# A spectral mixing layer in fp32 on one core: the first batch and the first tile written in program order, two tables split on the host

## The chip, the core and the metric

The kernel runs on one core of a Trainium2 chip. Times are device microseconds (us) of one execution. The trace is of one profiled execution; its times count from the start of its span. The engines are named as in the profile: PE (TensorE, matrix products), PEld (its weight loads), DVE (VectorE), ACT (ScalarE), POOL (GpSimd), SP (SyncE, which issues most transfers).

## What is computed

Two things in a row, for 8 batches of 576 tokens and a model width of 512 (8 heads of 64):

```python
p_packed = sm_attn(p, k, v)             # 32 packing queries per head attend to 576 keys
out = sm_attn(q, p_packed, p_packed)    # 576 queries attend to the 32 packed values
X = np.fft.fft(np.fft.fft(x, axis=1), axis=2)      # x: out with its heads side by side
u = x + np.real(X)
un = (u - mean(u)) / np.sqrt(var(u) + 1e-06)
return u + np.maximum(un @ w_ch1, 0.0) @ w_ch2     # 512 -> 2048 -> 512
```

## The kernel before

**The front and the tiles.** Each batch has a front (`front(b)`): the two softmaxes for two groups of four heads (g = 0, 1), then the two Fourier transforms as products with tables of cosines and sines, up to rows of `u` in the buffer `ubuf`. A batch gives 4.5 blocks of 128 rows, so that there are nine tiles of up to four blocks. Each tile goes through the two weight products (`ffn`): 16 chunks j, each with an `up` (24 instructions at the tile's start, since its first chunk is halved; 12 otherwise, `ph`, L647), a ScalarE pass `hh` (L653) and a VectorE pass `hl` (L654), which read the one PSUM bank of `ph`, and a `down` (12 products into four banks `acc`, L664), which runs one chunk later. After each `up` and each `down` comes a `step`, into which the front of the next batch is put piece by piece.

**Numbers in two parts.** Products run in a rounded format, so each operand x is a high part (a cast on ScalarE, L99) and a low part (x less the high part, L100), and a product is three (L237 to L239). The low parts of the weights, `wr_l`, are made on GpSimd anew in each tile.

**The weights' first load.** They come as 64-bit floats. A part (half a chunk: 128x512 of `w1f` or `w2f`) is put together by one ScalarE instruction (L179) and two of VectorE (a shift L180, a shift with an or L181). Chunks 0 and 1 are made ahead of the first tile, the others in its even steps, both parts of a chunk together. The first parts land in rows of `w1f` and `w2f` that are filled later (`STG0`), the others in turn in `ubuf` and a pair of buffers `wst`.

**What sets the order.** A program that adds a scheduler places the instructions of each engine by priority and dependency, except inside `manual_schedule`, where the order on PE, DVE, ACT and POOL is that of the program. Before, everything from the second tile on (t > 0) is inside, and the first batch's front and the first tile are outside. The transfers' order on SP is the scheduler's throughout. `ORDER[b]` is the order of the front's steps: K, V, Q are loads of keys, values and queries; s (scores of one group, S of both), t or X (turned scores), p, d (packed values and their parts), q or U (query scores), e, m, a (second softmax), g (spectrum of the values), f, r, h (folded weights, their remainder, their two parts). Batch 0 has an order of its own, batch 1 another, group by group, and from batch 2 on both groups go side by side. A table per batch (`EN`, `EF`, `ES`) says which of a step's passes run on VectorE (0) and which on GpSimd (1).

**After the fold.** The folded parts `fh` (ScalarE, L479) and `fl` (VectorE, L485) and the spectrum `gh`, `gl` go into 36 products `py` and `pyr` (L237 to L239), these into `pz` and `px`, and from there VectorE makes `pe`, `qe` and the four blocks of `ubuf` (L560 to L567). `statistics` takes a block's mean (L213, VectorE), its squares (`junk`, L217, ScalarE) and the deviation (L220, VectorE; L221, GpSimd). `Turned` takes the mean off (`un`, L601), transposes on PE (`untp`, L608) and splits into `uh` and `ul`; then the tile's first `ph` can start. The remainder of a batch's tokens (`R`: one more pair `pz`, `px` and `xa`, L581 to L584) comes after that.

**Tables.** `tabC`, `tabS`, `tabR` and `tabB` come as fp32 and are split or rounded in the kernel: L128, L129 (`basis`), L99, L100 (`tbh`, `tbl`), L141, L142 (`tbr`).

Of the kernel before, what the change touches and what calls it, by code (L numbers as in the profile page):

```python
# [9 lines left out]
F32 = mybir.dt.float32  # L10
# [6 lines left out]
P = 128  # L17
S = 576
# [13 lines left out]
ES = (1, 0, 0)  # L32
# [6 lines left out]
ORDER = ("K0 I0 K1 B0 V0 V1 Q0 Q1 W0 W1 W2 W3 s0 t0 p0 d0 s1 t1 p1 q0 e0 d1 g0 q1 e1 m0 m1 a0 f0 r0 h0 a1 "  # L39
         "f1 r1 h1 g1 T0",  # L40
         "s0 s1 y y t0 y t1 y p0 y y y d0 p1 y q0 d1 y y g0 y g1 y e0 q1 e1 y m0 y m1 y a0 a1 y f0 r0 h0 y "
         "y f1 r1 h1",
# [4 lines left out]
STG0 = [-2, -2, -4, -4, -6, -6]  # L47
STG1 = [9, None, None]
LEAD = 2
# [28 lines left out]
def tile_kernel(ctx, tc, kpT, qT, v, w1, w2, tabC, tabS, tabR, tabB, tabT, sel, ident_d, out):  # L78
# [45 lines left out]
    def load_base():  # L124
        nc.sync.dma_start(sels, sel)
        st = load(tabB, [P, 2, N2], "st_base", "wst")
        h = work.tile([P, 2, N2], F32R, tag="tmp", name="base_h", bufs=3)
        nc.scalar.copy(h, st)  # L128
        nc.vector.scalar_tensor_tensor(basis, h.bitcast(F32), selC, st, ALU.mult, ALU.add)  # L129
        nc.sync.dma_start(turn, tabT)  # L130

    def load_tables():
        for t, d in enumerate((tabC, tabS)):
            st = load(d, [P, 1, KT], "st_tab", (t, 2))
            split(tbh[t], tbl[t], st[:, 0, :])
        st = work.tile([P, 2, 320], F32, tag="wst", name="st_tabr", bufs=2)
        nc.sync.dma_start(st[:101], tabR)
        for t in range(2):

            h = work.tile([P, DM], F32R, tag="tmp", name="tabr_h", bufs=3)  # L140
            nc.scalar.copy(h[:101, :320], st[:101, t, :])  # L141
            nc.vector.scalar_tensor_tensor(  # L142
                tbr[t][:101], h[:101, :320].bitcast(F32), selA[:101], st[:101, t, :], ALU.mult, ALU.add)

    sels = cpool.tile([P, 3], F32, name="sels")
    selA, selB, selC = (sels[:, i:i + 1] for i in range(3))
# [9 lines left out]
    def fetch(j, n):  # L158
        i = stages.pop(0)
        if i is None:  # L160
            st = work.tile([P, 512, 2], I32, tag="wst", name="wst", bufs=2)
        elif i < 0:
            st = spot(n, i, [P, 512, 2]).bitcast(I32)
# [3 lines left out]
        fetched[j, n] = st  # L167

    def load_weights(j):

        for n, dst in enumerate((w1f, w2f)):
            if (j, n) not in fetched:
                fetch(j, n)
            st = fetched.pop((j, n))
            low, high = st[:, :, 0], st[:, :, 1]
            c = dst[:, j, :].bitcast(I32)


            nc.scalar.activation(c.bitcast(F32), high.bitcast(F32), AF.Prelu, scale=REBIAS, alpha=-2.0 ** 32)  # L179
            nc.vector.tensor_scalar(c, c, 3, None, ALU.logical_shift_left)  # L180
            nc.vector.scalar_tensor_tensor(c, low, 29, c, ALU.logical_shift_right, ALU.bitwise_or)  # L181
# [59 lines left out]
    def front(b):  # L241
# [31 lines left out]
        def scores(*gs):  # L273
# [9 lines left out]
            tails = now["acc"][2:] if len(gs) == 2 else {gs[0]: bank("s1t")}  # L283
# [161 lines left out]
        def folded_rest(g):  # L445
# [5 lines left out]
            sm = (nc.vector, nc.gpsimd)[ES[min(b, 2)]]  # L451
# [22 lines left out]
        def folded_parts(g):  # L474
# [15 lines left out]
                 "T": lambda _: load_tables(), "B": lambda _: load_base(), "K": load_keys, "V": load_values,  # L490
                 "Q": load_queries, "I": lambda _: nc.sync.dma_start(ident, ident_d),
                 "W": lambda i: fetch(i // 2, i % 2), "D": load_weights}
        for x in ORDER[min(b, 2)].split():
# [217 lines left out]
    gen0 = front(0)  # L711
    for at in gen0:
        if at == "rest":
            break
    cur = Turned(tiles[0][1])
    for i in range(4):
        cur.less(i)
        for move in cur.moves(i):
            move()
        cur.parts(i)  # L720
    for _ in gen0:
        pass
    spare.clear()
    rest = iter(())
    for j in range(ORDER[0].count("D"), LEAD):
        load_weights(j)
    ready, splits = [], wsplits()
    next(splits)
    next(splits)
    for t, (first, tk) in enumerate(tiles):  # L730

        gen = front(t + 1) if t + 1 < B else iter(())
        ended = []

        def step(i):

            next_step()
            if t > 0 and i in (0, 2):
                next(rest, None)
            elif not ended and next(gen, None) == "rest":  # L740
                ended.append(gen)
            if t == 0 and i % 2 == 0 and i // 2 + LEAD < NJ:
                load_weights(i // 2 + LEAD)
            assert i < 2 * NJ - 1 or t + 1 >= B or ended

        nxt = Turned(tiles[t + 1][1]) if t + 1 < len(tiles) else None

        with tc.manual_schedule(engines=MANUAL) if t > 0 else nullcontext():
            ffn(first, cur, step, nxt, t + 1 >= B)
        cur, rest = nxt, gen  # L750


def _tables():
# [98 lines left out]
```

## Time and profile before

| what | us |
|---|---|
| median of 3 runs (1027.23 to 1028.67) | 1028.21 |
| the profiled execution | 1027.14 |
| its span | 1025.3 |
| span up to the first `ph` of the first tile | 62.70 |
| first tile, first `ph` to the next tile's first `ph` | 126.18 |
| second tile, the same way | 108.95 |
| rest of the span after the first tile | 836.4 |

So 1.84 us lie around the span, and the profiled execution is 1.07 us below the median. PE is busy for 978.5 us (95%) of the span, DVE for 608.8, POOL for 463.1, ACT for 425.0.

How to read it: PE is all but full from the second tile on. Its idle time lies in the first 189 us, so that stretch has to be looked at by itself: which engine works there, and what PE waits for.

### The profile page before, as it was taken

To read this page: it belongs to the slowest core of one execution; us is meant where nothing else is said; L and a number is where in the kernel's file an instruction comes from. 1 tells how busy PE (TensorE), PEld (TensorE's weight loads), DVE (VectorE), ACT (ScalarE), POOL (GpSimd) and SP (SyncE) were. 2 spreads that over 40 slices of the span, in tenths; PEclk is the share of its full clock that TensorE was granted. 3 is DMA by queue.
4 is the path that set the end of the run, shared out by engine and by line. 5 is a ranking of instruction groups with operands and counts; after the bars stand their busy time and mean duration, and the time that the engine had idled before them with its cause. 6 is when DMAs were issued, how large, how long until landed. Compare 5 with 4: busy or idle time off the path is not lost.

```text
span 1025.3 us, 14876 instructions
## 1 busy us (share of the span) xinstructions
PE 978.5 (95%) x5692; PEld 795.6 (78%) x5692; DVE 608.8 (59%) x1264; ACT 425.0 (41%) x883; POOL 463.1 (45%) x419
## 2 busy tenths in 40 slices
PE   6489889999999999999999999999999999999998
PEld 2367668878877888788887887788778888887886
DVE  3897994559465856677556846594658562114112
ACT  2556454444443434444444435444435343333322
POOL 1535635364335534454345533643355344444443
PEclk9699899999999999999999999999999999999999
DMA  8328440220023000310041002200210000001001
GB/s 329 109 64 280 157 123 1 93 96 1 1 78 111 1 1 34 108 48 1 1 140 49 1 1 93 96 0 1 82 58 0 1 26 17 0 1 43 1 1 42
DMA packets 17742, 58.64 MB, mean 57 GB/s; under 512 B 2081, under 2 KB 2465, under 8 KB 17670
## 3 DMA queue, kind: packets, MB, share of 16 engines
q1 hardware_dynamic: 17670, 57.68, 16.4%
q8 instruction: 45, 0.74, 0.3%
q14 instruction: 27, 0.22, 0.1%
HBM read 48.24 MB, written 9.44 MB: 56 GB/s over the span
## 4 chain that ended last, share of the span: by engine, by line
PE 76%; DVE 11%; ACT 5%; DMA 3%; issue 2%; POOL 2%; ACTq 0%; SPq 0%; DVEq 0%; POOLq 0%
PE ph L647 35%; PE acc L664 30%; DVE ubuf L567 2%; DMA wst<-w 2%; DVE turned L419 1%; ACT hh L653 1%; PE po L326 1%; PE s L269 1%; ACT junk L217 1%; DVE turned L415 1%; POOL wr_l L100 1%; PE e1tp L303 1%; DVE hl L654 1%; ACT wr_h L99 1%; DVE w2f L181 1%
## 5 line engine op out<-in xcount | busy, mean ns | idle before, releaser
L100 POOL TENSOR_TENSOR wr_l<-w1f,wr_h 128x512 fp32r<-128x512 f32 x144 | 190.8, 1325 | 398.9 <-ACT wr_h L99 395.1
L654 DVE SCALAR_TENSOR_TENSOR hl<-ph,hh 128x512 fp32r<-128x512 f32 x144 | 98.8, 686 | 305.3 <-ACT hh L653 305.0
L647 PE MATMUL ph<-uh,wr_h 128*128 128x512 f32 (+1 forms) x580 | 231.5, 399 | 11.8 <-DVE hl L654 9.6
L100 POOL TENSOR_TENSOR wr_l<-w2f,wr_h 128x512 fp32r<-128x512 f32 x144 | 192.4, 1336 | 91.9 <-ACT wr_h L99 91.9
L664 PE MATMUL acc<-wr_l,hh 128*128 128x512 f32 x576 | 227.0, 394 | 3.0 <-POOL wr_l L100 3.0
L647 PE MATMUL ph<-uh,wr_l 128*128 128x512 f32 (+1 forms) x580 | 229.3, 395 | 0.4 <-POOL wr_l L100 0.4
L647 PE MATMUL ph<-ul,wr_h 128*128 128x512 f32 (+1 forms) x580 | 229.3, 395 | 0.2 <-DVE ul L100 0.2
L664 PE MATMUL acc<-wr_h,hh 128*128 128x512 f32 x576 | 227.8, 396 | 0.0
L664 PE MATMUL acc<-wr_h,hl 128*128 128x512 f32 x576 | 226.2, 393 | 0.0
L653 ACT ACTIVATE hh<-ph 128x512 fp32r<-128x512 f32 x144 | 85.8, 596 | 285.6 <-PE ph L647 285.4
L647 PEld LDWEIGHTS ph<-uh,wr_h 128*128 128x128 f32 x580 | 109.9, 190 | 44.9 <-DVE hl L654 9.8
L647 PEld LDWEIGHTS ph<-uh,wr_l 128*128 128x128 f32 x580 | 110.0, 190 | 24.7 <-POOL wr_l L100 0.8
L664 PEld LDWEIGHTS acc<-wr_l,hh 128*128 128x128 f32 x576 | 108.2, 188 | 26.8 <-POOL wr_l L100 5.4
L647 PEld LDWEIGHTS ph<-ul,wr_h 128*128 128x128 f32 x580 | 110.0, 190 | 23.9 <-issue 1.7
L664 PEld LDWEIGHTS acc<-wr_h,hh 128*128 128x128 f32 x576 | 108.2, 188 | 23.5 <-ACT w2f L179 0.8
L664 PEld LDWEIGHTS acc<-wr_h,hl 128*128 128x128 f32 x576 | 108.2, 188 | 23.1
L99 ACT CAST wr_h<-w2f 128x512 fp32r<-128x512 f32 x144 | 89.4, 621 | 9.4 <-PE ph L647 7.8
L99 ACT CAST wr_h<-w1f 128x512 fp32r<-128x512 f32 x144 | 88.4, 614 | 8.0 <-PE ph L647 3.1
L217 ACT ACTIVATE junk<-ubuf,stat 128x512 f32<-128x512 f32 x36 | 25.8, 718 | 77.3 <-DVE stat L213 77.3
L608 PE MATMUL untp<-ident,un 128*128 128x128 f32 x144 | 37.2, 273 | 1.9 <-DVE stat L220 1.7
L100 POOL TENSOR_TENSOR gl<-turned,gh 128x516 fp32r<-128x516 f32 x16 | 25.2, 1573 | 22.1 <-ACT gh L99 22.1
L567 DVE SCALAR_TENSOR_TENSOR ubuf<-qe,pe 128x512 f32<-128x512 f32 x32 | 34.6, 1115 | 0.5
(199 smaller groups left out, 1292.8 us busy)
## 6 DMA issues: line engine op xcount, KB each, us to landing
kp<-kpT SPq DMA_DIRECT2D x16, 608.0 KB, 4.9
out<-ubuf SPq DMA_DIRECT2D x36, 256.0 KB, 2.1
vt<-v SPq DMA_DIRECT2D x14, 640.0 KB, 4.7
wst<-w SPq DMA_DIRECT2D x17, 512.0 KB, 4.0
qt<-qT SPq DMA_DIRECT2D x14, 576.0 KB, 4.8
ubuf<-w SPq DMA_DIRECT2D x9, 512.0 KB, 4.6
w1f<-w SPq DMA_DIRECT2D x3, 512.0 KB, 11.1
w2f<-w SPq DMA_DIRECT2D x3, 512.0 KB, 11.2
```

Of the source, the lines that this page charges most:

```text
L99: nc.scalar.copy(hi, src)
L100: (lo_eng or nc.vector).tensor_tensor(lo, src, hi.bitcast(F32), ALU.subtract)
L181: nc.vector.scalar_tensor_tensor(c, low, 29, c, ALU.logical_shift_right, ALU.bitwise_or)
L217: nc.scalar.activation(junk, u, AF.Square, bias=st[:, 1:2], scale=-1.0, accum_out=st[:, 2:3])
L269: nc.tensor.matmul(res[g][c][at, :w.stop - w.start], lhs(g, h), rhs(g, h, w), start=True, stop=True, tile_position=(r, h * NPK))
L303: nc.tensor.transpose(tp[g][:, c * P:(c + 1) * P], e1s[g][:, c * P:(c + 1) * P], ident)
L567: nc.vector.scalar_tensor_tensor(u_of[key], qe, sign, pe, ALU.mult, ALU.add, accum_out=stat_of[key][:, 0:1])
L608: nc.tensor.transpose(tp[:, c * P:(c + 1) * P], un[:, c * P:(c + 1) * P], ident)
L647: nc.tensor.matmul(ph[:, t], l[:, c * P:(c + 1) * P], r[:, c, t], start=(k == 0), stop=(k == 11))
L653: nc.scalar.activation(hh[:, :T], ph[:, :T], AF.Relu)
L654: nc.vector.scalar_tensor_tensor(hl[:, :T], ph[:, :T], 0.0, hh[:, :T].bitcast(F32), ALU.max, ALU.subtract)
L664: nc.tensor.matmul(acc[i], l[:, w], r, start=(j == 0 and k == 0), stop=(j == NJ - 1 and k == 2))
```

## The change

Four things change together.

1. **The scheduler's part ends.** `manual_schedule` now spans everything, so that PE, DVE, ACT and POOL run the program's order from the first instruction on. Batch 0 gets an order of its own with both groups side by side, and batch 1 the one that all later batches have. `ES` is now per group: of batch 0, group 0's remainder is folded on POOL, group 1's on DVE.
2. **Tables.** High and low parts of the tables are made on the host. `basis`, `tbh`, `tbl` and `tbr` are loaded as they are, by seven transfers that POOL issues (an fp32 source into a rounded tile); six instructions of ACT and DVE for each kind go.
3. **Weights.** Parts are counted by one index m in the order of their use. Three are made ahead of the first tile, one in each of its steps: part i + 3 in step i, its transfer issued in step i - 2 (or, for nine, ahead of the tile). The high half (ACT) comes at the start of a step, the low half (DVE) at its end.
4. **The remainder of batch 0** moves into the first tile's steps 0 and 2, where later batches have it.

```diff
-ES = (1, 0, 0)
+ES = ((1, 0), (0, 0), (0, 0))
-ORDER = ("K0 I0 K1 B0 V0 V1 Q0 Q1 W0 W1 W2 W3 s0 t0 p0 d0 s1 t1 p1 q0 e0 d1 g0 q1 e1 m0 m1 a0 f0 r0 h0 a1 "
-         "f1 r1 h1 g1 T0",
+ORDER = ("K0 K1 I0 V0 V1 Q0 Q1 B0 L0 W0 W1 W2 W3 W4 W5 W6 W7 W8 S X p0 p1 d0 d1 U e0 e1 g0 g1 A0 m0 m1 a0 "
+         "a1 A1 f0 r0 h0 f1 r1 h1 D0",
-LEAD = 2
+LEAD = 3
     def load_base():
+        nc.gpsimd.dma_start(basis, tabB)
+        nc.sync.dma_start(turn, tabT)
+
+    def load_tables():
         nc.sync.dma_start(sels, sel)
         for t in range(2):
+            nc.gpsimd.dma_start(tbh[t], tabs[:, t, 0, :])
+            nc.gpsimd.dma_start(tbl[t], tabs[:, t, 1, :])
+            nc.gpsimd.dma_start(tbr[t][:101], tabR[:, t, :])
...
+    wparts = [(0, 0), (0, 1), (1, 0)] + [x for j in range(2, NJ) for x in ((j, 0), (j - 1, 1))] + [(NJ - 1, 1)]
...
+    def load_high(m):
+        if m < len(wparts):
+            j, n = wparts[m]
+            nc.scalar.activation((w1f, w2f)[n][:, j, :], fetched[m][:, :, 1].bitcast(F32), AF.Prelu,
+                                 scale=REBIAS, alpha=-2.0 ** 32)
+
+    def load_low(m):
+        if m < len(wparts):
+            j, n = wparts[m]
+            c = (w1f, w2f)[n][:, j, :].bitcast(I32)
             nc.vector.tensor_scalar(c, c, 3, None, ALU.logical_shift_left)
-            nc.vector.scalar_tensor_tensor(c, low, 29, c, ALU.logical_shift_right, ALU.bitwise_or)
+            nc.vector.scalar_tensor_tensor(c, fetched[m][:, :, 0], 29, c, ALU.logical_shift_right, ALU.bitwise_or)
...
-        for x in ORDER[min(b, 2)].split():
+        for x in ORDER[min(b, 1)].split():
...
+    def begin():
+        rest = front(0)
+        for at in rest:
+            if at == "rest":
+                break
+        next(splits)
+        cur = Turned(tiles[0][1])
+        for i in (0, 2):
+            for k in (i, i + 1):
+                cur.less(k)
+            for k in (i, i + 1):
+                for move in cur.moves(k):
+                    move()
+            for k in (i, i + 1):
+                cur.parts(k)
+        load_high(2)
+        load_low(1)
+        load_low(2)
+        next(splits)
+        spare.clear()
+        return cur, rest
...
+                if t == 0:
+                    if i + LEAD + 2 not in fetched:
+                        fetch(i + LEAD + 2)
+                    load_high(i + LEAD)
+                if i in (0, 2):
                     next(rest, None)
                 elif not ended and next(gen, None) == "rest":
                     ended.append(gen)
-            if t == 0 and i % 2 == 0 and i // 2 + LEAD < NJ:
-                load_weights(i // 2 + LEAD)
+                if t == 0:
+                    load_low(i + LEAD)
```

Three places show how rows move. The first is DVE at the end of batch 0's front, from the last pair of passes on the first two blocks (`ubuf`, with the numbers of the blocks' statistics) to the next blocks'. Before:

```order
L567 SCALAR_TENSOR_TENSOR ubuf_86,stat_515<-qe_512,pe_503 128x512
L567 SCALAR_TENSOR_TENSOR ubuf_86,stat_517<-qe_512,pe_503 128x512
L213 TENSOR_SCALAR stat_515<-stat_515 128x1
L181 SCALAR_TENSOR_TENSOR w2f_83<-w2f_83 128x512
L213 TENSOR_SCALAR stat_517<-stat_517 128x1
L601 TENSOR_SCALAR un_576<-ubuf_86,stat_515 128x512
L220 TENSOR_SCALAR stat_515<-stat_515 128x1
L560 TENSOR_TENSOR pe_550<-px_543,spec0_534 128x512
L220 TENSOR_SCALAR stat_517<-stat_517 128x1
L563 TENSOR_TENSOR qe_559<-px_552,spec1_541 128x256
```

And now (L208 and L215 are L213 and L220 of before):

```order
L562 SCALAR_TENSOR_TENSOR ubuf_86,stat_515<-qe_512,pe_503 128x512
L562 SCALAR_TENSOR_TENSOR ubuf_86,stat_517<-qe_512,pe_503 128x512
L208 TENSOR_SCALAR stat_515<-stat_515 128x1
L215 TENSOR_SCALAR stat_515<-stat_515 128x1
L208 TENSOR_SCALAR stat_517<-stat_517 128x1
L215 TENSOR_SCALAR stat_517<-stat_517 128x1
L555 TENSOR_TENSOR pe_550<-px_543,spec0_534 128x512
L558 TENSOR_TENSOR qe_559<-px_552,spec1_541 128x256
```

The mean of the second block and everything of the next two blocks now stand behind the first block's deviation; the passes `un` stand behind all four.

The second place is PE at the very start: scores (`s1t`, `s`), turned scores (`e1tq`, `e1tp`) and packed values (`po`) of batch 0. Before:

```order
L269 MATMUL s1t<-kp 32x64 x4
L269 MATMUL s_117<-kp 32x512 x4
L269 MATMUL s1t<-kp 32x64 x4
L306 MATMUL e1tq<-ident,e_131 64x128
L269 MATMUL s_186<-kp 32x512
L303 MATMUL e1tp<-ident,e_131 128x128 x4
L269 MATMUL s_186<-kp 32x512 x3
```

And now:

```order
L264 MATMUL s1t<-kp 32x64 x8
L264 MATMUL s_129<-kp 32x512
L264 MATMUL s_130<-kp 32x512
L264 MATMUL s_129<-kp 32x512
L264 MATMUL s_130<-kp 32x512
```

The two groups' products alternate, so that the first of them needs the keys of both groups.

The third place is DVE in the first tile, about its eighth to tenth chunk, around the passes `hl`. Before:

```order
L481 SCALAR_TENSOR_TENSOR xl<-eo,xh 128x256
L483 TENSOR_TENSOR ol<-eo,oh 128x256
L181 SCALAR_TENSOR_TENSOR w1f<-ubuf,w1f 128x512
L654 SCALAR_TENSOR_TENSOR hl<-ph,hh 128x512
L485 TENSOR_TENSOR fl<-f,fh 128x776
L180 TENSOR_SCALAR w2f<-w2f 128x512
L180 TENSOR_SCALAR w1f<-w1f 128x512
L181 SCALAR_TENSOR_TENSOR w2f<-wst,w2f 128x512
L100 TENSOR_TENSOR yl<-py,yh 128x258 x2
```

And now:

```order
L392 TENSOR_TENSOR s_1019<-s_1019,d_1226 128x576
L175 TENSOR_SCALAR w1f<-w1f 128x512
L176 SCALAR_TENSOR_TENSOR w1f<-wst,w1f 128x512
L420 TENSOR_TENSOR s_1019<-s_1019,z_1225 128x576
L422 STREAM_TRANSPOSE a<-s_1019 128x576
L175 TENSOR_SCALAR w2f<-w2f 128x512
L176 SCALAR_TENSOR_TENSOR w2f<-ubuf,w2f 128x512
L649 SCALAR_TENSOR_TENSOR hl<-ph,hh 128x512
```

Now two parts (L175 with L176, once each per step) stand between every two passes `hl`, up to step 28.

## Rows read from the trace of the kernel before

**Rows 1.** Busy time by stretch: length, busy us (instructions) per engine, granted clock, DMA.

```profile
0.00:62.70 62.70, 36.37 (x301) 24.59 (x301) 43.43 (x107) 28.61 (x66) 20.66 (x49) 0.84 0.52 183
62.70:188.88 126.18, 114.69 (x632) 89.87 (x630) 97.81 (x199) 61.27 (x122) 62.95 (x53) 0.95 0.38 125
188.88:297.83 108.95, 108.12 (x661) 88.95 (x660) 71.15 (x152) 47.12 (x100) 49.26 (x43) 1.00 0.13 45
```

**Rows 2.** Timeline, scores: start, duration, engine, line, operation, count [idle before <-releaser].

```profile
4.95 1.93 PE L269 MATMUL s<-kp 64*32 64x512 f32 x8
6.71 0.44 PE L269 MATMUL s1t<-kp 64*32 64x64 f32 x8
...
193.51 1.06 PE L269 MATMUL s<-kp 64*32 64x512 f32 x16
```

**Rows 3.** Timeline, TensorE, the last query scores of batch 0.

```profile
22.50 1.04 PE L269 MATMUL s2T<-w2f,ppT 64*32 64x512 f32 x8
```

**Rows 4.** Timeline, VectorE, batch 0: one of four spectrum products, the last fold.

```profile
20.84 0.70 DVE L415 TENSOR_TENSOR turned<-pg,turn 128x516 f32<-128x516 f32 x1 [0.35 <-PE pg L411]
...
44.49 0.97 DVE L485 TENSOR_TENSOR fl<-f,fh 128x776 fp32r<-128x776 f32 x1 [1.48 <-ACT fh L479]
```

**Rows 5.** Timeline, TensorE, the products after the fold: the first, the last, the next.

```profile
39.60 0.58 PE L237 MATMUL py<-gh,fh 128*128 128x258 f32 x1 [15.12 <-ACT fh L479]
...
48.76 0.42 PE L239 MATMUL py<-gh,fl 128*128 128x258 f32 x1
48.97 0.42 PE L237 MATMUL pyr<-gh,fh 128*99 128x258 f32 x1
...
49.37 0.28 PE L239 MATMUL pyr<-gh,fl 128*99 128x258 f32 x1
49.49 0.28 PE L237 MATMUL pz<-yh,tbh 128*128 128x258 f32 x1
```

**Rows 6.** Timeline, end of batch 0's front: statistics of a block, the first tile's start.

```profile
60.19 0.15 DVE L213 TENSOR_SCALAR stat<-stat 128x1 f32<-128x1 f32 x1
...
61.06 0.19 ACT L217 ACTIVATION_READ_ACCUMULATOR junk<-ubuf,stat 128x1 f32 x1
...
62.70 0.36 PE L647 MATMUL ph<-uh,wr_h 128*128 128x256 f32 x1
```

**Rows 7.** Waits of TensorE in the first tile: us in total, times, longest.

```profile
PE ph L647 <- DVE hl L654: 9.6, 3, 4.4
```

**Rows 8.** Groups by line, VectorE, 70 to 188 us: busy, mean ns, idle before.

```profile
L180 DVE TENSOR_SCALAR w2f<-w2f 128x512 int32<-128x512 int32 x14 | 9.0, 641 | 4.3 <-ACT w2f L179 4.3
...
L180 DVE TENSOR_SCALAR w1f<-w1f 128x512 int32<-128x512 int32 x13 | 7.2, 551 | 2.7 <-ACT w1f L179 2.7
L181 DVE SCALAR_TENSOR_TENSOR w2f<-wst,w2f 128x512 int32<-128x512 int32 x9 | 8.6, 955 | 0.2
...
L181 DVE SCALAR_TENSOR_TENSOR w1f<-ubuf,w1f 128x512 int32<-128x512 int32 x5 | 3.4, 688 | 0.1
```

**Rows 9.** Timeline of a later tile, VectorE and one TensorE row, chunks without a wait.

```profile
453.40 0.69 DVE L397 TENSOR_TENSOR s<-s,d 128x576 f32<-128x576 f32 x1
454.13 0.76 DVE L425 TENSOR_TENSOR s<-s,z 128x576 f32<-128x576 f32 x1
...
455.63 0.65 DVE L654 SCALAR_TENSOR_TENSOR hl<-ph,hh 128x512 fp32r<-128x512 f32 x1
...
457.37 0.39 PE L647 MATMUL ph<-uh,wr_h 128*128 128x512 f32 x1
...
461.64 1.45 DVE L437 TENSOR_TENSOR eo<-a 128x287 f32<-128x287 f32 x1
...
465.30 0.54 DVE L455 TENSOR_TENSOR f<-eo 128x45 f32<-128x45 f32 x4
...
477.49 0.68 DVE L654 SCALAR_TENSOR_TENSOR hl<-ph,hh 128x512 fp32r<-128x512 f32 x1
```

**Rows 10.** The table `turn`, its one transfer from SP: us from issue to landing.

```profile
DMA to landing us min/median/max: 5.9/5.9/5.9
```

More of the change, by code (lines that the diff above doesn't have):

```diff
@@ L124, in load_base @@
     def load_base():
[L125 to L129, printed above, removed]
+        nc.gpsimd.dma_start(basis, tabB)
         nc.sync.dma_start(turn, tabT)
     def load_tables():
[L133 to L137, printed above, removed]
-        for t in range(2):
[L140 to L148, printed above, removed]
+        nc.sync.dma_start(sels, sel)
+        for t in range(2):
+            nc.gpsimd.dma_start(tbh[t], tabs[:, t, 0, :])
+            nc.gpsimd.dma_start(tbl[t], tabs[:, t, 1, :])
+            nc.gpsimd.dma_start(tbr[t][:101], tabR[:, t, :])
+    sels = cpool.tile([P, 1], F32, name="sels")
+    selB = sels[:, 0:1]
     fetched = {}
@@ L280, in keys_of @@
                 return kps[g][side(g, h):side(g, h) + D, h // 2, w]
-            tails = now["acc"][2:] if len(gs) == 2 else {gs[0]: bank("s1t")}
+            tails = now["acc"][2:] if b > 0 else {g: bank("s1t") for g in gs}
             sc = narrow(gs, lambda g, h: keys_of(g, h, slice(S, S + NPK)), keys_of, "s1", tails)
@@ L709, in tile_kernel @@
     tiles = [(i, keys[i:i + 4]) for i in range(0, len(keys), 4)]
[L711 to L726, printed above, removed]
-    ready, splits = [], wsplits()
-    next(splits)
@@ L729, in tile_kernel @@
[L729 to L741, printed above, removed]
-            if t == 0 and i % 2 == 0 and i // 2 + LEAD < NJ:
-                load_weights(i // 2 + LEAD)
-            assert i < 2 * NJ - 1 or t + 1 >= B or ended
-        nxt = Turned(tiles[t + 1][1]) if t + 1 < len(tiles) else None
-        with tc.manual_schedule(engines=MANUAL) if t > 0 else nullcontext():
+    ready, splits = [], wsplits()
@@ new lines, in tile_kernel, with step @@
+    with tc.manual_schedule(engines=MANUAL):
+        cur, rest = begin()
+        for t, (first, tk) in enumerate(tiles):
+            gen = front(t + 1) if t + 1 < B else iter(())
+            ended = []
+            def step(i):
+                next_step()
+                if t == 0:
[3 more added lines that the diff above has]
+                if i in (0, 2):
+                    next(rest, None)
+                elif not ended and next(gen, None) == "rest":
+                    ended.append(gen)
+                if t == 0:
+                    load_low(i + LEAD)
+                assert i < 2 * NJ - 1 or t + 1 >= B or ended
+            nxt = Turned(tiles[t + 1][1]) if t + 1 < len(tiles) else None
@@ L749, in tile_kernel @@
             ffn(first, cur, step, nxt, t + 1 >= B)
-        cur, rest = nxt, gen
+            cur, rest = nxt, gen
 def _tables():
@@ L812, in _prepare @@
     }
[L813 removed]
+    for n, t in zip(("tabs", "tabR", "tabB", "tabT", "sel", "ident_d"), _tables()):
         arrays[n] = t
```

50 lines of the change are left out of this document (24 added, 26 removed).

## The prediction

> **What bounds the kernel now.** I read the stretches first [rows 1]. From the first tile's end on nothing is to be had: the second tile takes 108.95 us with TensorE busy for 108.12, and the change leaves every row there as it is. The 836.4 us behind the first tile are taken as they are. The first two stretches hold the loss: 62.70 us up to the first `ph`, in which VectorE works for 43.43 and TensorE for 36.37, and a first tile of 126.18, 17.2 longer than the second. The timeline then says who holds TensorE. In the front it is the chain through VectorE: TensorE idles 15.12 us until the first folded part is there [rows 5], and it then runs at the lower of its two levels (1.2 GHz): one product starts 0.21 us after the other at 48.76, and 0.12 after it at 49.37 [rows 5]. In the first tile it is `hl`, 9.6 us in three waits [rows 7]: `ph` has one bank, and the next `up` waits until VectorE has read it. The rest of the 17.2 is slow clock around these waits (granted share 0.95, [rows 1]).
>
> So there are two terms: the first `ph` moves, and the first tile becomes a tile like the others with weight parts in it.
>
> **The change part by part.**
>
> *First `ph`, step 1: to the query scores.* Before, they end at 23.54 [rows 3]. Now the first product waits for both groups' keys, 6.71 instead of 4.7; in return 16 products of both groups take as long as 8 (1.06 us for 16 at the fast level, 1.93 for 8 at the slow one [rows 2]). At best the whole 1.93 is won, at worst nothing, because group 0 no longer runs ahead. I take the middle: 22.6.
>
> *Step 2: to the last `fl`.* Before it ends at 45.46 [rows 4], 21.9 after the query scores, with VectorE all but full. Now all four spectrum products stand behind the query scores, where two stood ahead of them: 2 x 0.70 [rows 4] = 1.4. Smaller rows change sides, each under 1 us by its duration: group 0's query transposes and group 1's remainder come in, a weight shift and the wait for GpSimd's second remainder go out. I take +1.1 for these, between -1.5 and +2. The last `fl` ends at 22.6 + 21.9 + 1.4 + 1.1 = 47.0. The rows on the tables cost nothing here: they ran after this point, under TensorE's products.
>
> *Step 3: `py`.* In program order the sixth product already needs group 1's `fl`, so 31 of 36 are left at 47.0. At 0.21 each that is 6.5, at 0.12 it is 3.7. Before, TensorE had idled, took up work at 39.60 and came to the fast level near 49.4. It will have idled longer here; I let it turn fast at 51.5: 21 products in 4.5 and 10 in 1.2, end at 52.7 (50.7 to 53.5). Before: 49.65.
>
> *Step 4: from there to `ph`.* Before 13.05 us. Now, with `after` at work only inside tiles, each block's statistics stand in line: mean, squares on ScalarE, deviation, then the next block. One block takes 60.19 to 61.25 [rows 6] and some 0.15 to hand over, 1.2. The chain, counted from the last `pyr`: last split and both `pz` 2.0, `pe`, `qe` and the first two blocks 2.75, so 4.75; two statistics 2.4, 7.15; the next `pz` copies stand behind ScalarE's squares, then the same passes again, 2.95, 10.1; two statistics, 12.5; `un` of blocks 0 and 1 and their transposes, split on ScalarE and VectorE, then `un` of 2 and 3, which stand behind the second `ul`: 4.5, 17.0; their transposes, with TensorE having idled for 8 us and so slow, 1.9, 18.9. (All products of that step stand ahead of the first `ph`.) The scheduler had laid the weight shifts, `xa` and `un` between these. `xa` and its two followers leave this stretch and come back inside the tile, where every later tile has them in its 108.95; nothing is booked twice.
>
> First `ph`: 52.7 + 18.9 = 71.6, **8.9 later**. Bounds: 50.7 + 17 = 67.7 to 53.5 + 20.5 = 74. The first `up` then starts slow: 24 half products at 0.21 instead of 0.12 would be 2.2; I take 1.0.
>
> *First tile.* Without parts it would take 108.95. In it 29 parts are put together. VectorE's two rows have means of 0.55 to 0.64 and 0.69 to 0.96 in the first tile before [rows 8], together 1.24 to 1.60; since rows start about 0.15 before their forerunner's end, 1.1 to 1.45 in a row, and I take 1.30. The whole is 38 us, and a later tile leaves VectorE 108.95 - 71.15 = 37.8 [rows 1]. But the room isn't where the parts are. Between 450.0 and 477.5 of a later tile, five chunks, VectorE never waits: `hl` follows on the row before it [rows 9], and TensorE runs at its 5.44 per chunk. Its only slack is that `hl` at 455.63 ends 1.1 before the next `ph` at 457.37 [rows 9]. Ten parts fall there, 13.0 us. Batch 1 has some of that work on GpSimd, as before: two scalings of group 0 (0.69 and 0.76) and its fold, 461.64 to 465.30 = 3.7 [rows 9], together 5.2. Left: 13.0 - 5.2 - 1.1 - 0.2 of idle = **6.5 us of waits**. At 1.1 a part it is 4.5, and below that if the collisions with GpSimd fall on other rows. If GpSimd comes late with its steps so that VectorE waits for them, the 5.2 don't count: 11.7. The waits are of 1 to 2.5 us, and after waits of 4 us TensorE's clock fell before; I take 1.2 for slow stretches. The tile: 108.95 + 6.5 + 1.2 = 116.65, **9.5 less** than 126.18.
>
> ScalarE's part of this (one row per part, under 0.7) is hidden: it is busy for 47.12 of 108.95 [rows 1]. It now stands ahead of `hh` in ScalarE's order, so a late transfer would hold `hh` and TensorE behind it; a part's transfer has two steps, some 6.8 us.
>
> *Tables.* Seven transfers are issued by GpSimd ahead of its first work in the front, which comes near 16.5 us. The trace has no transfer from GpSimd. The nearest row is SyncE's `turn`, 5.9 from issue to landing [rows 10]: if GpSimd only issues, the price is nothing, if it were held for each landing, 41 us, with its first work 25 late. I take nothing, since SyncE's own issues follow each other without waiting for landings.
> The Trainium skill (SBUF — State Buffer, SBUF: two separate sides) has a rule against such a move: a transfer issued by GpSimd needs descriptors written through a port that VectorE's two-port passes lock, and it gives 3.1 us for one that alone takes 0.62. No run here shows a transfer under such a lock; by that figure seven would end near 22 and the sum would be some 6 us longer.
>
> **The sum.** Span: 71.6 + 1.0 + 116.65 + 836.4 = 1025.65, 0.35 more than 1025.3. With the 1.84 around the span the profiled execution would take 1027.5; the median of runs lies 1.07 above the profiled one, so **1028.6**. About 0.2% (2.1 us) is what a measurement of this kernel can tell from no change, so this is no change: two terms of nine us against each other.
>
> **The rivals.**
>
> *Fewer collisions, faster.* If VectorE and GpSimd meet less than taken, both terms shrink: a pass like the one at 461.64 takes 1.45 where its twins without GpSimd take a third. For: group 1's remainder leaves GpSimd in the front. Against: in the first tile GpSimd has more to do than in later ones. Step 2 at 45.4, `py` to 51.0, `ph` at 69.9 (+7.2), first `up` +0.5; the tile with 3 of waits and 0.4 of slow clock 112.35 (-13.8): 6.1 less, **1022.1**.
>
> *VectorE's line holds the first tile, slower.* One mechanism, in the eighth to twelfth chunk: in program order VectorE waits at its transpose `a` for GpSimd's scaling of group 0, which stands behind two `wr_l`, and ten parts queue behind that. For: no slack there in a later tile [rows 9]. Against: before, batch 1 had the same division. Waits 11.7, slow clock 2.5, tile 123.15 (-3.0); with +8.9 and +1.0 it is 6.9 more, **1035.1**. It decides from waits of about 8 us on.
>
> *GpSimd's transfers hold its first work.* Priced above: 25 us, some 1054. For: nothing in the trace; that SyncE issues freely speaks against.
>
> **How the numbers follow.** Forecast 0.38, collisions 0.33, line 0.26, transfers 0.03. Of the forecast's 0.38, some 0.08 lie outside the 0.2%, half on each side. So faster 0.37, within 0.2% 0.30, slower 0.33. The range reaches down past the second case by 2 (step 1 and step 3 at their low ends) and up past the third by 2: 1020 to 1037. The likeliest case's own range is 1025 to 1032.
>
> **What would show it.** The first `ph` near 71.6 us, four statistics in a row with VectorE idle on ScalarE's squares ahead of it, and `py` still slow at 50. In the tile: waits for `hl` in the eighth to twelfth chunk, of 6 us in sum and 1 to 2.5 each, none of over 4. The prediction is wrong if the first `ph` comes before 67 (steps 2 to 4) or after 75, if the first tile is under 112 or over 122, or if a later tile leaves 108.95.

## The result, and the profile after

The changed kernel takes 1031.63 us in the median of six runs (1031.27 to 1033.40), the kernel before 1028.55 on the same chip (1027.23 to 1029.06, six runs). The ratio is 1.0036 with a 95% interval of 1.0023 to 1.0049: slower by more than the 0.2% that can be told from no change. The forecast of 1028.6 was no change, with a range of 1020 to 1037.

Two terms of several us stand against each other, as forecast, though both came out smaller (8.9 later and, with the slow first `up`, 8.5 shorter were forecast). The busy times by stretch (length, busy us and instructions of PE, PEld, DVE, ACT, POOL, granted clock, DMA share, GB/s) answer to [rows 1]:

```profile
69.98:192.03 122.05, 113.26 (x674) 91.97 (x673) 105.57 (x201) 64.83 (x131) 59.80 (x52) 0.97 0.41 130
192.03:301.00 108.97, 108.16 (x662) 88.95 (x661) 71.90 (x153) 47.14 (x100) 50.34 (x44) 1.00 0.13 45
0.00:69.98 69.98, 28.59 (x257) 21.36 (x257) 40.93 (x110) 23.07 (x52) 21.71 (x44) 0.73 0.46 168
```

The first `ph` comes 7.28 us later (69.98 after 62.70), the first tile is 4.13 shorter (122.05 after 126.18), so that the second tile starts 3.15 later, which is the whole difference of the medians. The profiled execution took 1031.47 and is 4.33 above that of before; the other 1.2 us lie behind the first tile (837.67 after 836.42), where no chunk is more than 0.06 us longer and half of it comes behind the last `up`. In the traces of the experiments below this stretch takes 836.8 to 837.7, so that the profiled run of before was at its low end, and nothing points to the change there.

The front, in the timeline of after (start, duration, engine, line; L208 and L215 are L213 and L220 of before, L596 is L601, L642 is L647), to be read beside [rows 3 to 6]:

```profile
19.83 1.05 PE L264 MATMUL s2T<-w2f,ppT 64*32 64x512 f32 x1
...
45.40 0.97 DVE L480 TENSOR_TENSOR fl<-f,fh 128x776 fp32r<-128x776 f32 x1 [0.24 <-ACT fh L474]
...
49.16 0.42 PE L234 MATMUL pyr<-gh,fl 128*101 128x258 f32 x1
...
49.69 0.28 PE L234 MATMUL py<-gh,fl 128*128 128x258 f32 x1
...
51.48 0.28 PE L234 MATMUL pyr<-gh,fl 128*99 128x258 f32 x1
...
56.68 0.15 DVE L208 TENSOR_SCALAR stat<-stat 128x1 f32<-128x1 f32 x1
57.77 0.15 DVE L215 TENSOR_SCALAR stat<-stat 128x1 f32<-128x1 f32 x1 [0.94 <-ACT junk L212]
58.87 0.15 DVE L215 TENSOR_SCALAR stat<-stat 128x1 f32<-128x1 f32 x1 [0.88 <-ACT junk L212]
59.13 0.69 DVE L555 TENSOR_TENSOR pe<-px,spec 128x512 f32<-128x512 f32 x1
...
64.00 0.87 DVE L596 TENSOR_SCALAR un<-ubuf,stat 128x512 f32<-128x512 f32 x2
64.62 1.94 PE L603 MATMUL untp<-ident,un 128*128 128x128 f32 x8 [7.65 <-DVE un L596]
...
69.98 0.56 PE L642 MATMUL ph<-uh,wr_h 128*128 128x256 f32 x1
```

VectorE waits for ScalarE's squares ahead of each deviation (0.94 and 0.88 in the first pair, the same in the second), and TensorE has been idle for 7.65 us when the transposes start.

The waits of TensorE in the first tile of after (us in total, times, longest) answer to [rows 7]:

```profile
PE ph L642 <- ACT wr_h L97: 6.3, 3, 2.5
PE ph L642 <- DVE s L369: 1.4, 1, 1.4
PE ph L642 <- DVE hl L649: 0.6, 1, 0.6
PE acc L659 <- POOL wr_l L98: 0.5, 1, 0.5
```

The first row has to be read with care. It names ScalarE's `wr_h`; the timeline around the first of the three waits, with the first rows of the other two, shows who really came last for `ph`:

```profile
125.48 0.69 DVE L176 SCALAR_TENSOR_TENSOR w2f<-wst,w2f 128x512 int32<-128x512 int32 x1
126.09 0.68 DVE L649 SCALAR_TENSOR_TENSOR hl<-ph,hh 128x512 fp32r<-128x512 f32 x1
126.26 0.62 ACT L97 CAST wr_h<-w2f 128x512 fp32r<-128x512 f32 x1 [2.11 <-DVE w2f L176]
126.92 0.47 PE L642 MATMUL ph<-uh,wr_h 128*128 128x512 f32 x1 [1.76 <-ACT wr_h L97]
...
134.69 0.63 PE L642 MATMUL ph<-uh,wr_h 128*128 128x512 f32 x1 [2.05 <-ACT wr_h L97]
...
149.96 0.47 PE L642 MATMUL ph<-uh,wr_h 128*128 128x512 f32 x1 [2.50 <-ACT wr_h L97]
```

This `wr_h` is made from `w2f`, which `ph` doesn't read. `hl` ends at 126.77, and `ph` starts 0.15 later; at the wait that the profile does give to `hl` (113.66) the distance is 0.14, and at the other two of these waits it is 0.14 and 0.15 as well. Both `hl` and `wr_h` had waited for the same weight part. So the waits are for `hl`, in all four cases.

### The profile page after: what moved, and what is told of

Same layout as the page of the kernel before. It is cut to its first block, busy times and chain, and to the rows that moved or that the text cites. A ratio compares the mean times of both kernels' runs of the same rounds, so it can differ in the third digit from the quotient of the medians.

```text
span 1029.7 us, 14881 instructions
## 1 busy us (share of the span) xinstructions
PE 970.0 (94%) x5692; PEld 794.6 (77%) x5692; DVE 615.2 (60%) x1271; ACT 423.2 (41%) x878; POOL 463.5 (45%) x414
## 4 chain that ended last, share of the span: by engine, by line
PE 79%; DVE 11%; ACT 4%; issue 3%; POOL 2%; DMA 0%; SPq 0%; ACTq 0%; POOLq 0%; DVEq 0%
PE ph L642 36%; PE acc L659 31%; DVE ubuf L562 2%; DVE turned L414 1%; ACT hh L648 1%; ACT junk L212 1%; PE po L321 1%; DVE turned L410 1%; POOL wr_l L98 1%; PE py L234 1%; PE e1tp L298 1%; PE untp L603 1%; PE s L264 1%; PE py L232 1%; PE py L233 1%
## 5 line engine op out<-in xcount | busy, mean ns | idle before, releaser
L642 PE MATMUL ph<-uh,wr_h 128*128 128x512 f32 (+1 forms) x580 | 231.4, 399 | 10.2 <-ACT wr_h L97 6.3
L642 PE MATMUL ph<-uh,wr_l 128*128 128x512 f32 (+1 forms) x580 | 229.0, 395 | 0.0
L642 PE MATMUL ph<-ul,wr_h 128*128 128x512 f32 (+1 forms) x580 | 228.8, 394 | 0.0
L642 PEld LDWEIGHTS ph<-uh,wr_h 128*128 128x128 f32 x580 | 110.2, 190 | 44.8 <-ACT wr_h L97 7.5
L642 PEld LDWEIGHTS ph<-uh,wr_l 128*128 128x128 f32 x580 | 110.1, 190 | 24.2 <-POOL wr_l L98 0.2
L642 PEld LDWEIGHTS ph<-ul,wr_h 128*128 128x128 f32 x580 | 110.2, 190 | 21.7
L232 PE MATMUL py<-gh,fh 128*128 128x258 f32 x64 | 19.0, 298 | 20.8 <-ACT fh L474 20.8
L98 DVE TENSOR_TENSOR ul<-untp,uh 128x512 fp32r<-128x512 f32 x36 | 24.1, 687 | 20.4 <-ACT uh L97 20.4
```

The lines of the kernel that those rows point to most:

```text
L98: (lo_eng or nc.vector).tensor_tensor(lo, src, hi.bitcast(F32), ALU.subtract)
L232: nc.tensor.matmul(o, lh, rh, start=first, stop=False)
L642: nc.tensor.matmul(ph[:, t], l[:, c * P:(c + 1) * P], r[:, c, t], start=(k == 0), stop=(k == 11))
```

## The experiments

In what follows, a wait is sized by the distance from one `up` or `down` to the next, beside the same distance in the second tile, and j counts the chunks from 0. In after the first tile is 13.1 us longer than the second:

| where | us more |
|---|---|
| first `up` and the steps up to the second | 2.0 |
| ahead of j = 4, query transposes | 1.1 |
| `hl`, ahead of j = 6, 8, 9, 11, with the products right after | 0.9, 2.3, 2.2, 2.8 |
| the slow `up` of j = 9 | 1.7 |

In the first row, the first `up` takes 4.45 us up to the next step's first product, 1.7 more than in the second tile, at a granted clock of 0.62. But the clock isn't what sets this row: in e2_stats_un (below) the first `up` takes 3.6, and the second still comes 7.38 after the first instead of 7.67. The score products between them wait in both: seven of the sixteen start together 0.05 to 0.06 us behind the end of ScalarE's first copy `spec` (76.63 after 76.58 in after, 70.29 after 70.23 in e2_stats_un), which speaks for ScalarE's line; no run takes that line away.

The theory: the front is late because statistics stand in line, and the tile is longer by weight parts that stand in front of `hl` where VectorE is full. The rivals: the front hangs on TensorE's clock and on the line of splits; the tile hangs on VectorE's waits for GpSimd.

**Statistics put off (e1_stats).** Of the kernel after, with

```diff
+        if steps[0] is None:
+            due.append((2 + key[2], squares))
+            due.append((4 + key[2], deviation))
+            return
         after(1, squares)
```

> The changed kernel, with squares and deviations of batch 0's first four blocks put off into steps 1 to 4 of the first tile (the means stay). Theory (statistics in line): the second pair's pe, now at 59.13 us, starts at 56.9, and un, now at 64.0, another 2.1 earlier: the first ph comes at 65.7 us (65 to 66.5) instead of 69.98, the first tile stays at 122 (up to 123 if the squares hold hh on ScalarE), the span falls by 4.3 (3.3 to 4.7). Rival (the slow TensorE and the line of splits on ScalarE and VectorE set that stretch, the statistics only fill its gaps): first ph not before 68.5, span less by under 1.5.

Measured: first `ph` at 65.97, first tile 121.8, 1027.20 us (ratio to before 0.9989, 0.9976 to 1.0002), 4.4 less than after. The theory holds, to 0.3 us.

**`un` moved up (e2_stats_un).**

```diff
             for k in (i, i + 1):
                 for move in cur.moves(k):
                     move()
-            for k in (i, i + 1):
+            if i == 0:
+                continue
+            for k in range(4):
                 cur.parts(k)
```

> As e1_stats, and un of blocks 2 and 3 with their transposes stands ahead of the splits uh, ul of blocks 0 and 1. Theory: the second eight transposes now start 3.7 us after the first eight (68.36 and 64.62), because un 2 stands behind the second ul; they will start some 1.8 after. First ph 1.9 earlier than in e1_stats, at 63.8 (63.2 to 64.6), span 1.9 less than e1_stats. Rival (ScalarE's four uh in a row hold the first ph): gain under 0.7.

Measured: all 16 transposes now run as one group, and the first `ph` is at 63.92:

```profile
61.09 3.18 PE L607 MATMUL untp<-ident,un 128*128 128x128 f32 x16 [3.34 <-DVE un L600]
...
63.92 0.56 PE L646 MATMUL ph<-uh,wr_h 128*128 128x256 f32 x1
```

1025.46 us (0.9975, 0.9963 to 0.9987). These two edits give back 6.1 of the 7.3 us.

**Twelve parts left out (e4_leave).** VectorE's two instructions are not issued for the parts of steps 12 to 23, so that those weights lack their low bits.

```diff
-                if t == 0:
+                if t == 0 and not 12 <= i <= 23:
                     load_low(i + LEAD)
```

> The changed kernel, with VectorE's two instructions left out for the parts of steps 12 to 23 (their low bits are missing from the weights; transfers and ScalarE's half stay). Theory: no wait for hl from chunk 7 on, no slow clock there: tile 112.5 us (111.5 to 113.5). Rival (GpSimd's steps or the transfers hold the line): tile 117 or more.

Measured, in one execution: first tile 114.77, 7.3 less, no wait for `hl` behind j = 6 and no slow `up`.

```profile
PE acc L659 <- POOL wr_l L98: 1.6, 2, 1.1
PE ph L642 <- DVE hl L649: 0.6, 1, 0.6
```

It stayed above the expected 113.5 since a wait came forth that had been hidden: 1.1 us for GpSimd's `wr_l`, in the `down` ahead of j = 10. So twelve parts cost 7.3 us there, not 12 x 1.3, and what is left to GpSimd's lateness alone (the rival) is this 1.1.

**Parts made earlier in the tile (e3_early).** The place of each part comes from a list: one more in steps 1, 3, 5, 7, 9, none in 12 to 16.

```diff
-                    load_low(i + LEAD)
+                    for m in PLAN[i]:
+                        load_low(m)
```

> The changed kernel, with the same parts made earlier: one more part in each of steps 1, 3, 5, 7 and 9, none in steps 12 to 16, so that seven instead of twelve parts fall into steps 12 to 23 (transfers land in four more places). Theory (VectorE is full there, each part costs its 1.3 us): in chunks 6 to 11 TensorE's waits for hl, 8.2 us more than in the second tile plus 1.7 of slow clock, fall to 2 and 0; the tile takes 114.5 us (113 to 117) instead of 122.05. Rival (VectorE's line held by GpSimd's late steps in the eighth to tenth chunk, whatever parts stand there): tile 119 or more. Rival (extra parts in the early chunks cost what they save later): 120 to 123.

Measured: 1031.44 us (1.0031, 1.0017 to 1.0045), the time of after; the profiled run was the longest of its ten (1035.37), and in its trace the tile takes 125.5. The theory's number fell. By the median the tile is as long as in after, which is the last rival's number (120 to 123); the trace's own 125.5 lies above it, and the first rival's 119 or more is not set apart by either (e4_leave does that). The waits of the tile in that trace show why:

```profile
PE ph L652 <- ACT wr_h L107: 2.8, 2, 2.4
PE ph L652 <- DVE hl L659: 2.7, 1, 2.7
PE acc L669 <- POOL wr_l L108: 1.6, 2, 1.1
PE s2Tt L274 <- DMA qt<-qT: 1.3, 1, 1.3
PE ph L652 <- DVE s L379: 1.0, 1, 1.0
```

The 2.7 us wait is now ahead of j = 6, behind the added parts: chunks 3 to 5 had no room either. And pulling the weights' transfers forward made the queries of batch 1 land late.

**Parts made in the front's gaps (e5_plan).** On e2_stats_un, six parts ahead of the tile, one more in steps 0 to 3, none in 9 and 12 to 18.

```diff
+            if n < 2:
+                load_low(n + 1)
...
-        load_high(2)
-        load_low(1)
-        load_low(2)
+        for m in (3, 4, 5):
+            load_low(m)
```

> As e2_stats_un (first ph 63.92, first tile 122.92), with the weight parts moved to where VectorE waits: parts 1 and 2 behind the two yr of batch 0's front, 3 to 5 behind the last ul, so that the tile starts with six parts made; then one per step, one more in steps 0 to 3, none in steps 9 and 12 to 18 (transfers land in four more places). Theory (waits come from parts in full stretches, chunks 6 to 11; the early room is in the front and in chunks 0 and 1, not in chunks 3 to 5 where e3_early put them): first ph 63.9 (63.5 to 64.5), first tile 115 (113.5 to 117), time 1017.5. Rival (VectorE is as full in the early chunks, what is saved late is paid early): tile 119 or more, a wait of over 2 us in chunks 2 to 5.

Measured: 1027.02 us (0.9988, 0.9978 to 0.9999), first `ph` 65.32, first tile 122.5, as long as without the plan. The rival's number (119 or more) came, but not its mechanism: not one wait for `hl` is left, and others have taken their place.

```profile
PE acc L673 <- POOL wr_l L108: 3.1, 4, 1.1
PE po L335 <- DMA vt<-v: 2.2, 1, 2.2
PE ph L656 <- DVE s L383: 1.4, 1, 1.4
```

The values of batch 1 landed late, behind weight parts: SyncE issues five between 69.26 and 78.69 and the second half of the values at 79.11, where in after none is issued from 50 us until both halves of the values are (77.78). And TensorE's granted clock was 0.63 in the 4.6 us after that wait (4.0 us in all). The parts of the last chunks, now two steps ahead of their use instead of three, came just late (3.9 us, around j = 11 and in the last two chunks).

**The clock in the front (e6_warm, e11_warm_py).** Products that nobody reads fill TensorE's idle time.

```diff
+        for _ in range(n):
+            nc.tensor.matmul(o[:, :256], lhs, rhs, start=True, stop=True)
```

> As e2_stats_un, with 157 more products on TensorE whose results nobody reads, in its idle stretches of batch 0's front: 110 behind the spectrum products, 22 behind xh of group 0, 25 behind the last px. Theory (the low clock level after idling costs py, the transposes and the first up): py at 0.12 us instead of 0.21 a product, its end at 50.3 instead of 52.53, transposes and first up at the fast level, first ph at 61.3 (60.5 to 62), first up 4.6 instead of 5.35, span 3.4 less (2.5 to 4.5). Rival (these stretches hang on VectorE and ScalarE, TensorE's level is covered): first ph 63.3 or later, span less by under 1. Rival (the added products run at the low level and hold py): first ph later than 64.5.

Measured: first `ph` at 63.08, 0.8 earlier, and 1025.79 us (0.9976, 0.9966 to 0.9986), the time of e2_stats_un. That is far from the theory's 61.3 and close to the first rival's 63.3: `py` was still slow for the most part, because TensorE idled again between the two groups' folded parts:

```profile
45.69 0.58 PE L236 MATMUL py<-gh,fh 128*128 128x258 f32 x1 [2.23 <-ACT fh L483]
...
47.07 0.42 PE L236 MATMUL py<-gh,fh 128*128 128x258 f32 x1
47.28 0.42 PE L237 MATMUL py<-gl,fh 128*128 128x258 f32 x1
```

So the next kernel fills this wait too, with 17 more.

> As e6_warm, with 17 more unread products in the 2 us in which TensorE waits between group 0's and group 1's folded parts, where its clock fell again in e6_warm. Theory (with the level up, the 18 products from 46.7 on that still took 0.21 us take 0.12): py's last product ends at 50.6 instead of 52.42, first ph at 61.4 instead of 63.08, time 1.7 less. Rival (behind py the line of VectorE and ScalarE sets the time anyway): first ph 62.5 or later.

```profile
43.16 2.18 PE L243 MATMUL fill<-xh,pph 128*128 128x256 f32 x17
45.57 0.39 PE L236 MATMUL py<-gh,fh 128*128 128x258 f32 x1 [0.23 <-ACT fh L483]
...
46.92 0.28 PE L237 MATMUL py<-gl,fh 128*128 128x258 f32 x1
47.03 0.28 PE L238 MATMUL py<-gh,fl 128*128 128x258 f32 x1
...
50.26 0.28 PE L238 MATMUL pyr<-gh,fl 128*99 128x258 f32 x1
```

Measured: one product starts 0.12 us after the other, the last ends at 50.54, the first `ph` is at 61.21; 1023.45 us (0.9955, 0.9941 to 0.9968). The theory holds: the low level in `py` cost 1.9 us of the front.

**The front left to the scheduler (e7_schedfront).**

```diff
-    with tc.manual_schedule(engines=MANUAL):
-        cur, rest = begin()
+    cur, rest = begin()
+    with tc.manual_schedule(engines=MANUAL):
```

> The changed kernel, with batch 0's front left to the scheduler (same order of emission), and only the first tile and what follows in program order. Theory (the front loses 7.3 us to program order, above all to the statistics in line; the tile's gain is independent of it): first ph 63 us (62 to 64.5), first tile 122 (121 to 123.5), time 1024 (1022.5 to 1026). Rival (the two groups side by side make the front late, however it is ordered): first ph 67 or later, time 1028 or more.

```profile
57.62:184.00 126.38, 115.69 (x681) 94.15 (x682) 106.86 (x209) 65.58 (x133) 60.00 (x54) 0.96 0.38 126
```

Measured: 1021.75 us (0.9937, 0.9922 to 0.9953), faster than before and after. The first `ph` came at 57.62, earlier than expected, because the scheduler put the first five of the 24 products of the first `up` ahead of the transposes of blocks 2 and 3; the tile's length isn't comparable for that. The second tile's start is: 184.00, against 192.03 for after and 188.88 for before. So the program order of the front costs 8.0 us (9.9 by the medians; the profiled run was the longest of its four), and the rest of the change gains 4.9 (6.2 by the medians, 1027.99 of before and 1021.75).

**Tables alone (e8_tables).** The kernel before, with the tables of after.

> The kernel before with only the tables changed: parts made on the host, seven transfers issued by GpSimd, the rows of basis, tbh, tbl and tbr gone from ScalarE and VectorE. Theory (they ran beside TensorE's products): first ph 62.7 within 0.7, time within 2 us of before. Rival (VectorE's 3.3 us of tbl and tbr, 45.4 to 48.5, hold the first yl and all behind it): first ph 60 to 61.5, time 1.5 to 3 less. Rival (transfers from GpSimd hold its first work): first ph 64 or later.

Measured: 1027.19 us over ten runs (0.9991, 0.9976 to 1.0006): no change that can be told. The profiled run is the fastest of the ten (1024.11), so its first `ph` at 61.76 decides nothing within 1 us. That leaves the rival on VectorE's 3.3 us (1.5 to 3 less) open: the interval reaches down to 2.5 less. In after's trace the rival on GpSimd's transfers is out: issuing one takes 0.5 to 0.8 us, and GpSimd's first work on the front starts when VectorE's `pp` releases it.

```profile
1.26 0.79 POOL L123 DMA_DIRECT2D basis<-tabB  x1 [0.43 <-issue]
...
5.25 0.55 POOL L131 DMA_DIRECT2D tbr<-tabR  x1
...
15.13 0.61 POOL L329 TENSOR_TENSOR bd<-pp,bmask 128x256 f32<-128x256 f32 x1 [9.33 <-DVE pp L326]
```

**A better plan for the parts (e9_sched_plan, e10_sched_plan_b).** Both on e7_schedfront, with six parts in the front, transfers of parts 9 to 12 issued there, and a lead that never falls under 4. They differ in which steps get a second part and which none: (0, 1, 2) and (12, 13, 14, 15, 18) in e9, (0, 1) and (13, 15, 17, 19) in e10.

> As e7_schedfront (batch 0's front left to the scheduler, first tile in program order; first ph 57.62, first down 68.15, second tile's first ph 184.0), with six parts made in the front, one more part in each of steps 0, 1 and 2, and none in steps 12 to 15 and 18, so that the lead never falls under 4; the transfers of parts 9 to 12 are issued in the front, where the queues are idle. Theory (a wait for hl shrinks by 1.3 us for each part taken out of the two steps ahead of it, and without waits of 2 us the clock stays up): the waits ahead of chunks 8 and 9 go (4.5), the one ahead of chunk 11 halves (1.3), 1.7 of slow clock goes: second tile at 176.5 (175.5 to 179), time 1014.5 (1013 to 1017). Rival (as in e5_plan, VectorE running ahead makes others late: batch 1's values land late, GpSimd's low parts, the last weights): 181 or later, time 1018.5 or more.

> As e9_sched_plan, but one more part in steps 0 and 1 only, and none in steps 13, 15, 17 and 19: every chunk from the seventh to the tenth is relieved of one of its two parts instead of some of both. Theory (each part is worth its 1.3 us where the wait is longer than that): the waits ahead of chunks 8, 9 and 11 shrink by 1.3 each (3.9), slow clock 1.7 goes: second tile at 178.4 (177.5 to 180), time 1016. Rival (others become late): 181 or later.

Measured: e9 1019.73 us (0.9921, 0.9908 to 0.9933), second tile at 180.91; e10 1019.19 us (0.9913, 0.9900 to 0.9927), second tile at 179.94. e10's second tile came into its range at the edge (177.5 to 180), but its time is 3.2 above the expected 1016; e9 fell short by 4.4, near its rival's 181. The waits of e9 ahead of j = 8 and 9 are gone, but there the values land 1.2 us late again, and TensorE waits 1.8 us for a `wr_l` that GpSimd reaches later; e10 has that wait too (1.7).

```profile
82.27 0.90 PE L331 MATMUL po<-vt,e1T 128*32 128x64 f32 x40 [1.23 <-DMA vt<-v]
...
128.68 0.50 PE L669 MATMUL acc<-wr_l,hh 128*128 128x512 f32 x1 [1.76 <-POOL wr_l L108]
```

e10 beats the kernel before by 0.87%.

**Parts in pairs (e12_pairs).** Undoes the spreading over half chunks: both parts of a chunk in the even step, four ahead of the tile. (In this kernel one of the last parts is overwritten in its landing place before it is read, so that half a chunk of weights is wrong; this lies behind the waits spoken of.)

```diff
-                if t == 0:
-                    load_low(i + LEAD)
+                if t == 0 and i % 2 == 0:
+                    load_low(i + 4)
+                    load_low(i + 5)
```

> The changed kernel, with both parts of a chunk made in the even steps, as the kernel before had it, in place of one part in each step (four instead of three ahead of the tile; more places for the transfers, issued two steps ahead as in the changed kernel, so that none lands late). Theory (what counts is VectorE's work between two hl, and two steps, so two parts, stand between them either way): first ph 70 (69.5 to 70.7), first tile 122 (120.5 to 123.5), time 1031.4 within 1.5. Rival (two parts in a row hold hl as they did before, in waits of about 4 us): tile 125 or more, time 1034 or more.

Measured: 1037.91 us (1.0100, 1.0077 to 1.0123), first `ph` 70.20, first tile 128.1. The theory fell, the rival's number held, though not by waits of 4 us for `hl`. The largest wait is for the query transposes, ahead of j = 4, in front of which now two parts stand:

```profile
100.94 0.41 DVE L176 TENSOR_SCALAR w1f<-w1f 128x512 int32<-128x512 int32 x1
101.39 0.69 DVE L177 SCALAR_TENSOR_TENSOR w1f<-w2f,w1f 128x512 int32<-128x512 int32 x1
101.99 1.50 DVE L176 TENSOR_SCALAR w2f<-w2f 128x512 int32<-128x512 int32 x1
103.53 0.69 DVE L177 SCALAR_TENSOR_TENSOR w2f<-w1f,w2f 128x512 int32<-128x512 int32 x1
104.13 0.37 DVE L370 STREAM_TRANSPOSE s<-s2Tt 128x64 f32<-128x64 f32 x2
...
104.52 0.61 PE L643 MATMUL ph<-uh,wr_h 128*128 128x512 f32 x1 [3.59 <-DVE s L370]
```

`hl` isn't the only pass that TensorE waits for: the tail of the query scores lies in `ph`'s bank too. Behind it the clock fell (1.6 us in that `up`, 1.5 in that of j = 6). So, in program order, one part per half chunk is worth some 6 us of the first tile.

## Why the prediction was right, and where not

| step | predicted | measured |
|---|---|---|
| 1, query scores end | 22.6 | 20.88 |
| 2, last `fl` ends | 47.0 | 46.37 |
| 3, last `py`, `pyr` ends | 52.7 | 51.76 |
| 4, from there to the first `ph` | 18.9 | 18.2 |
| first `ph` | 71.6 | 69.98 |
| first tile, with the slow first `up` | 117.65 | 122.05 |
| rest of the span | 836.4 | 837.67 |

*Step 1* was out of its bounds: it is 2.7 us earlier than before, where 1.93 was the most thought possible. The bound took only the products; with both groups side by side their passes on VectorE and ScalarE come closer together as well: ScalarE's first pass `e` of group 1 starts 1.0 us after that of group 0 (10.51 after 9.54), before 6.7 (14.64 after 7.99).

*Step 2* lost what step 1 had won: 25.5 us after the query scores, where 24.4 was predicted, just over the upper bound of 25.3. That the two came out only 0.6 early together is luck: the errors, -1.7 and +1.1, stand against each other.

*Step 3* was right in that `py` starts at the low level, which e11_warm_py prices at 1.9 us. But the clock rose at 49.4, as in before, though TensorE had idled longer (18.78 us instead of 15.12); the 51.5 that was put in for this, and the sign that `py` is still slow at 50, did not come.

*Step 4* was right, in size and cause: 18.2 for 18.9, and its inner marks (the first two blocks, each pair of statistics, the second `un`) lie within 0.3 us of the sum's. e1_stats takes 4.0 us off with the statistics alone, e2_stats_un another 2.1 with `un` that stood behind `ul`.

*First tile.* It took 122.05, just over the 122 that the prediction had named as the sign of being wrong. The kind of the waits was right: four waits for `hl`, idle for 0.6 to 2.5 us each, none over 4, the last three ahead of j = 8, 9 and 11. The tile is 4.4 longer than forecast; sized as above, these rows hold it but for 0.1:

| term | predicted | measured |
|---|---|---|
| waits for `hl` in the eighth to twelfth chunk | 6.5 | 7.3 |
| wait for `hl` ahead of j = 6 | 0 | 0.9 |
| wait for the query transposes ahead of j = 4 | 0 | 1.1 |
| slow clock behind the waits | 1.2 | 1.7 |
| first `up` and the steps behind it | 1.0 | 2.0 |

So the balance over the five full chunks was 0.8 off. The step that failed is that the waits were looked for in these five alone, as if the other chunks, which have room in sum, could have none: 2.0 us came there. A wait comes from the work ahead of one particular pass. Inside the five chunks too, nothing was waited for ahead of j = 7 and 10, and over 2 us each ahead of j = 8, 9 and 11; e3_early and e12_pairs made waits of 2.7 and 3.6 us ahead of j = 6 and 4 by parts put there. The term for the first `up` was half the measured size, and its cause, the slow clock, accounts for 0.3 of the 2.0 by e2_stats_un.

How the parts come to cost what they do can be seen in VectorE's and GpSimd's rows of after:

```profile
115.01 1.46 POOL L98 TENSOR_TENSOR wr_l<-w2f,wr_h 128x512 fp32r<-128x512 f32 x1 [0.95 <-POOL wr_l L98]
115.34 1.68 DVE L176 SCALAR_TENSOR_TENSOR w1f<-wst,w1f 128x512 int32<-128x512 int32 x1
117.46 0.69 DVE L176 SCALAR_TENSOR_TENSOR w2f<-wst,w2f 128x512 int32<-128x512 int32 x1
```

The same pass takes 0.69 alone and 1.68 when GpSimd has begun a pass of its own; it then ends 0.55 us after GpSimd's (117.02 after 116.47, and likewise 0.55 at 112.92 and 122.87). The Trainium skill (SBUF — State Buffer, Who interferes with whom) says that a VectorE instruction with two inputs in SBUF contends with a GpSimd instruction that reads SBUF, and that the later one is blocked until the other is done; these rows agree.

*Rivals.* Fewer collisions did not come: its first `ph` of 69.9 was met (69.98), but by other steps than its own, and its tile of 112.35 was not. VectorE's line held by GpSimd's scaling: VectorE did wait at the transpose `a`, once, for 1.1 us, but without the parts no wait for `hl` remained from j = 7 on (e4_leave), so this isn't what decided. GpSimd's transfers held nothing.

The time was 3.0 us above the forecast: -1.6 in the front, +4.4 in the first tile, +1.3 in the rest of the span, and -1.0 because the median lay 0.16 instead of 1.07 above the profiled execution and 1.77 instead of 1.84 lay around its span. It lies between the likeliest case and the rival at 1035.1, and within the likeliest case's own range of 1025 to 1032. "Slower", which had 0.33, came and not "within 0.2%", which had 0.30: the two terms, 7 and 4 us against each other, were sized too loosely to tell the sign, so that no more than the range can be counted as foreseen.

The rule of the Trainium skill on GpSimd's transfers (SBUF — State Buffer, SBUF: two separate sides) has not been put to the test by any run here: in after, up to 6.79 us VectorE ran nothing but one memset while the seven were issued.

## What to carry to other kernels

Program order at a kernel's cold start has to be written for the start, not taken over from the steady state: a helper that spreads its steps over later slots inside the loop ran them in line where there were no slots, and that alone cost 4 us. Work that is put into a full engine's queue is priced by the pass that stands behind it, not by the engine's idle time in sum; and when it is moved, the transfers that move with it, and the engine that then gets its work later, can take back the gain: all of it in two of the four plans here that made parts earlier (e3_early, e5_plan), a part of it in the other two. Where a profile gives a wait to an engine, look whether the waiting instruction reads what that engine made at all.

## What the runs showed that had not been expected

- The clock does not follow the length of one wait. In after a wait of 2.05 us (ahead of j = 9) was followed by an `up` at the lower level, one of 2.50 (ahead of j = 11) by an `up` at the upper one. In e6_warm a wait of 2.23 was followed by 19 slow products, though TensorE had been at the upper level for the 20 us before (granted clock 1.00 from 22 to 42 us, busy for 16.95 of them); in the 3.70 us from 42.0 on it was busy for 0.60.
- Kernels whose front and first tile are the scheduler's spread more than most of those in program order: before ran from 1025.16 to 1031.65 in the 27 runs taken beside e5_plan to e8_tables, e8_tables itself from 1024.11 to 1030.78 in ten; e2_stats_un from 1023.82 to 1026.33 and e6_warm from 1024.96 to 1026.27 in ten each. It isn't a rule: e3_early, in program order too, ran from 1030.84 to 1035.37 in ten. Why, no run here tells.
